# One V load ahead of the sums' weights, a copy moved to ScalarE, and another opening, in a fused attention and mixture kernel

## The chip, the core and the metric

The kernel runs on one NeuronCore of a Trainium2 chip. The core has five engines that run their own instruction streams and meet at semaphores: TensorE (PE in the profile; its weight loads are PEld), VectorE (DVE), ScalarE (ACT), GpSimd (POOL) and SyncE (SP). POOL and SP also issue DMA transfers. POOL's transfers go through one software queue (q0 in the profile), SP's through one hardware queue (q1); both run on the same 16 DMA engines. The metric is the device time of one execution in microseconds (us).

## The reference

Two stages are computed, the second from the first:

```python
# attention: 8 batches, 8 heads, 512 local and 32 global tokens, head size 64
out_g = softmax(q_g @ [k_g, k_l]^T / 8) @ [v_g, v_l]           # a global row sees everything
out_l = softmax([q_l @ k_g^T, q_l @ k_l^T within 32 rows] / 8) @ [v_g, v_l]
x = concat(out_g, out_l) as 4352 tokens x 512

# mixture: 8 experts, all of them for every token, weighted by P
P = exp(x @ w_gate - max)
8 times: P /= rows' sums; P /= columns' sums; P *= N / E
out = sum over e of P[:, e] * (relu(x @ w1[e]) @ w2[e])         # w1: 512 x 1024, w2: 1024 x 512
```

## The kernel before

**Slots.** Attention runs in 34 slots, s = 0 to 33 (the loop at L453). Slot s belongs to batch b = s // 4 and pair of heads hp = s % 4. Each slot issues pieces of several pairs in an order written out by hand, and each engine runs its own pieces in exactly that order:

- `st_A(s+1)` (L249) transposes q and k of the next pair on TensorE; VectorE copies k out of PSUM (`kTe`), ScalarE copies q (`qbd`).
- `st_B(s, part)` (L266), three parts: scores on TensorE, mask and row maximum on VectorE, exponential on ScalarE into `Pu`. Each row has 128 columns of a local window and 32 for the global tokens.
- `st_D1(s-1)` (L292): VectorE copies the 32 global columns of `Pu`, which lie strided, into `Pl` (L295); TensorE transposes the other 128; VectorE copies them to `pw` (L300).
- `st_D2` (L302): TensorE transposes `Pl`, and the finished rows `xn` of an earlier pair; ScalarE copies both out, the second into `xT`, the tokens for the mixture.
- `st_E(s-1)` (L319): probabilities times V on TensorE. Even blocks of 64 rows read `va`, odd ones `vb`, and the global part reads `vgz`.
- `st_G1` to `st_G4`: the same for the global rows.

From slot 5 on each slot also does a part of the mixture for experts 0 and 1: four pieces of the first layer (`p_l1`, L408) and from slot 8 two of the second (`p_l2`, L422). After each fourth piece of the second layer SP stores one megabyte (`yd<-yst`, L436). After the loop come the rest of experts 0 and 1, the balancing of P, and experts 2 to 7, computed with seven products of half size in place of eight (`Slot`, `Unit`); this last part takes from about 395 us to the end.

**V.** For each batch `load_v` (L152) returns five steps. The first loads the global V into DRAM as fp16 (`vg16`) and the first part of `va`; three more load `va[:, 1]` to `va[:, 3]`, all on POOL's queue; the last loads the end of `vb` and then issues, on SP's queue, three copies from `va` to `vb` (L166 to L168, the moves) and four small loads of `vgz` (`load_vz`, L150). The moves wait until what they read of `va` has landed, L167 for all four parts. `va`, `vb` and `vgz` have two buffers each, so batch b + 1 is loaded while batch b is computed; it is first needed at `st_E(4(b+1))`, in slot 4(b+1) + 1.

**The sums.** Experts 2 to 7 need sums and differences of blocks of their weights. In the 24 slots from 8 on, `sums_load` (L95) loads one weight matrix as fp16 (`pw`, 1 MB) in an even slot and `sums_form` (L102) forms four blocks on POOL in the odd slot after it (L113, four instructions) and stores them in DRAM (`kept<-psum`). There is one buffer `pw`, and POOL runs in order: load, wait, form, store, and so on. hp 0 and 1 have a first-layer matrix, hp 2 and 3 a second-layer one.

**The queue of loads.** The list `queue` holds steps for POOL. It is filled at hp 0 with four loads of the next batch's q and k, and at hp 2 with the five steps of V. From slot 8 on two steps are taken in hp 0 and in hp 1, three in hp 2 and the rest in hp 3. In hp 2 the sums' load is issued after the three steps, and in hp 3 the two last steps come before `sums_form`. So POOL's own order for a batch is: store of the sums, `vg`, three parts of `va`, `pw`, the fourth part of `va`, the end of `vb`, wait and form, store, q, k, `pw`, q, k, wait and form. Up to slot 7 everything in the queue is taken at once.

**The opening.** In slot 0 the global queries are cast (`cast_g`) and transposed (`transpose_g`, 4 products) before the second part of slot 0's scores is done. In slot 4 two pairs' rows `xn` are transposed, the second (`st_D2(None, 1)`, L524) ahead of `st_A(5)`.

Of the kernel before, what the change touches and what calls it, by code (L numbers as in the profile page):

```python
# [11 lines left out]
FP32 = mybir.dt.float32  # L12
# [11 lines left out]
def kernel(  # L24
# [13 lines left out]
    nc = tc.nc  # L38
# [5 lines left out]
    P = 128  # L44
# [5 lines left out]
    NJ = Sl // P  # L50
# [5 lines left out]
    KW = P  # L56
# [63 lines left out]
    with ExitStack() as att:  # L120
# [31 lines left out]
        def load_v(b):  # L152
            va, vb = vab[b % 2]
            vz = vgz[b % 2]
            src = v_l[b].rearrange("h s d -> s h d")

            def first():
                nc.gpsimd.dma_start(out=vg16[b], in_=v_g[b].rearrange("h g d -> g h d"))
                nc.gpsimd.dma_start(out=va[W:P, 0, :, 0:Dh], in_=src[0:96])

            def mid(j):
                nc.gpsimd.dma_start(out=va[:, j, :, 0:Dh], in_=src[P * j - W : P * j + 96])

            def last():
                nc.gpsimd.dma_start(out=vb[HB : HB + W, NJ - 1, :, 0:Dh], in_=src[Sl - W : Sl])
                nc.sync.dma_start(out=vb[96:P, NJ - 1], in_=va[W : 2 * W, 0])  # L166
                nc.sync.dma_start(out=vb[0:HB, :], in_=va[HB:P, :])  # L167
                nc.sync.dma_start(out=vb[HB:P, 0 : NJ - 1], in_=va[0:HB, 1:NJ])  # L168
                if b > 1:
                    load_vz(b)  # L170

            return [first] + [lambda j=j: mid(j) for j in range(1, NJ)] + [last]

        gst = {}

# [14 lines left out]
        def cast_g(tg):  # L190
            t, fv = gst[(0, tg)]
            nc.vector.tensor_copy(out=t, in_=fv)
            gst[(0, tg)] = t
# [55 lines left out]
        def st_A(n):  # L249
            b, hp = divmod(n, HP)  # L250
            qs, ks = staged[b]
            qb, kt = qbd[n % 2], kTe[n % 4]
            pt = ps_tr.tile([P, 2, Sl], FP16, tag="tr")
            for t, src in enumerate((ks, qs)):
                for so in range(NJ):
                    for a in range(2):
                        nc.tensor.transpose(pt[HB * a : HB * (a + 1), t, P * so : P * (so + 1)],  # L257
                                            src[:, 2 * hp + a, so, :], identity)
            nc.vector.tensor_copy(out=kt[:, W : W + Sl].rearrange("c (p s) -> c p s", s=NJ),
                                  in_=pt[:, 0, :].rearrange("c (s p) -> c p s", s=NJ))  # L260
            for a in range(2):
                r = slice(HB * a, HB * (a + 1))
                nc.scalar.copy(out=qb[r, :, HB * a : HB * (a + 1)].rearrange("c i (p s) -> c i p s", s=NJ),
                               in_=pt[r, 1, :].rearrange("c (s i p) -> c i p s", s=NJ, i=NHB))
# [27 lines left out]
        def st_D1(n):  # L292
            d = st[n]
            d["Pl"] = att_wk.tile([P, NHB, Sg], FP16, tag="Pl", name="Pl")
            nc.vector.tensor_copy(out=d["Pl"], in_=d["Pu"][:, :, KW:SW])  # L295
            ptw = ps_tr.tile([P, NHB, P], FP16, tag="tr")
            for i in range(NHB):
                nc.tensor.transpose(ptw[:, i, :], d["Pu"][:, i, 0:KW], identity)  # L298
            d["pw"] = att_wk.tile([P, NHB, P], FP16, tag="pw", name="pw")
            nc.vector.tensor_copy(out=d["pw"], in_=ptw)  # L300

        def st_D2(n, n2):  # L302
            tgx = ps_tr.tile([P, 6, P], FP16, tag="tr")
            if n2 is not None:
                b, hp = divmod(n2, HP)
                xn = st[n2]["xn"]
                for j in range(NJ):
                    nc.tensor.transpose(tgx[:, 2 + j, :], xn[:, j, :], identity)
            if n is not None:
                d = st[n]  # L310
                for t in range(2):
                    nc.tensor.transpose(tgx[:, t, :], d["Pl"][:, 4 * t : 4 * t + 4, :], identity)
                d["pg"] = att_wk.tile([P, 2, P], FP16, tag="pg", name="pg")
                nc.scalar.copy(out=d["pg"], in_=tgx[:, 0:2, :])
            if n2 is not None:
                nc.scalar.copy(out=xT[:, hp, Sl * b : Sl * (b + 1)], in_=tgx[:, 2:6, :].rearrange("p j q -> p (j q)"))
                del st[n2]
# [120 lines left out]
        def load_first():  # L438
            wts[0] = [load_w1(0)]
            nc.gpsimd.dma_start(out=wg_sb, in_=moe_w_gate.rearrange("(dko dki) e -> dki dko e", dki=P))  # L440

        queue = []
        NU = B * HP
        for t in range(2):
# [8 lines left out]
        for s in range(NU + 2):  # L453
            b, hp = divmod(s, HP)
            if s < NU and b + 1 < B:
                if hp == 0:
                    queue = load_qk(b + 1, 0, 4, H)
                if hp == 2:
                    queue += load_v(b + 1)
                if s == 4:  # L460
                    queue += [lambda: wts.__setitem__(1, [load_w1(1)]), lambda: wts[0].append(load_w2(0))]
                if s == 5:
                    queue += [lambda: load_g(1, "kgs"), lambda: load_g(1, "qgs")]
                if s == 7:
                    queue += [lambda: wts[1].append(load_w2(1))]
                take = 0 if s == 0 else len(queue) if s < 8 else 2 if hp < 2 else 3 if hp == 2 else len(queue)
                if s == 1:
                    queue += [load_first]
                    take = len(queue)
                for i, f in enumerate(queue[:take]):  # L470
                    f()
                    if s == 2 and i == 0:
                        load_vz(1)
                queue = queue[take:]

            if 8 <= s < 8 + 4 * (E - 2):
                i, late = divmod(s - 8, 2)
                (sums_form if late else sums_load)(2 + i // 2, i % 2)

            l1, l2 = [], []  # L480
            if s >= 5:
                pieces = range(4 * (s - 6) + 2, 4 * (s - 6) + 6)
                l1 = [(i // FT % 2, i // FT // 2, i % FT) if i >= 0 else None for i in pieces]
            if s >= 6:
                k, hf = divmod(s - 6, 2)
                if k >= 1:
                    l2 = [((k - 1) % 2, (k - 1) // 2, 2 * hf + i) for i in range(2)]
            n1 = n2 = 0

            def f1(eng):  # L490
                nonlocal n1
                if n1 < len(l1):
                    if l1[n1]:
                        p_l1(*l1[n1], eng)
                    n1 += 1

            def f2(eng):
                nonlocal n2
                if n2 < len(l2):
                    p_l2(*l2[n2], eng)  # L500
                    n2 += 1

            g_odd = s % 2 == 1 and 3 <= s <= NU + 1
            if g_odd:
                gb, gg = divmod((s - 3) // 2, 2)
            even = s % 2 == 0 and 2 <= s <= NU
            f1("a")
            if s < NU:
                st_B(s, 0)
            if even:  # L510
                st_G1(*divmod((s - 2) // 2, 2))
            if 1 <= s <= NU:
                st_D1(s - 1)
            if s == 3:
                st_E(1)
            if g_odd:
                st_G2(gb, gg)
            f2("a")
            if s < 7:
                st_B(s, 1)  # L520
            if 1 <= s:
                st_D2(s - 1 if s <= NU else None, s - 2 if s >= 4 else 0 if s == 3 else None)
            if s == 4:
                st_D2(None, 1)  # L524
            if 7 <= s < NU:
                st_B(s, 1)
            f1("a")
            if s + 1 < NU and s < 7:
                st_A(s + 1)
            if s == 0:  # L530
                cast_g("qgs")
                transpose_g(0, "qgs")
            f1("v")
            if s < NU:
                st_B(s, 2)
            if s + 1 < NU and s >= 7:
                st_A(s + 1)
            if s == 2:
                st_E(0)
            if 3 <= s <= NU:  # L540
                st_E(s - 1)
            f2("a")
            if s >= 6 and (s - 6) % 4 == 0:
                logits(NJ * ((s - 6) // 4), NJ)
            if g_odd:
                st_G3(gb, gg)
            if s == 8:
                transpose_g(1, "kgs")
                transpose_g(1, "qgs")
            if s == 18:  # L550
                st_G4(0)
            f1("a")
        logits(NJ * (B - 1), NJ)


# [445 lines left out]
```

## Time and profile before

| what | value |
|---|---|
| median of 3 runs | 1041.32 us (1039.04 to 1042.68) |
| the profiled execution | 1041.35 us, span 1039.6 us, mean granted clock 0.99 |
| PE busy | 997.0 us, 96% of the span |
| ACT, DVE busy | 654.7 us, 760.7 us |
| POOL busy | 260.9 us, 25% |
| q0 (POOL's queue) | 87.32 MB, 103776 packets |
| chain that ended last | PE 80%, DMA 9%, POOL 5% of the span |

The span is what the engines' records cover; the execution's own time has 1.75 us more around it. Busy time of PE counts pipelined products with modelled ends, so 96% does not mean that PE is at its peak. The waits say more: for each instruction they give what released it. The chain goes back from the last instruction, step by step, to whatever it had waited for.

### The profile page before, as it was taken

The page shows a single profiled execution, that of the slowest core. Times are in us where ns is not written, and L with a number is a line of the kernel's source. Part 1 is how long each engine was busy: PE and PEld are TensorE (multiplying, and loading weights), DVE is VectorE, ACT ScalarE, POOL GpSimd, SP SyncE. Part 2 cuts the span into 40 slices and gives each one's busy share as a digit, 9 for nine tenths or more (in the row PEclk, how much of TensorE's full clock was granted, in tenths as well). Part 3 has the DMA queues.
Part 4 walks back from the last instruction along what each step waited for, and adds up shares of the span by engine and source line. Part 5 has one row for each costly group of instructions (what it writes and reads, how often), then busy time and mean ns, then how long its engine had stood idle before and what let it go on. Part 6 is the DMA issues. An engine that isn't in the chain of part 4 may idle for free.

```text
span 1039.6 us, 21929 instructions
## 1 busy us (share of the span) xinstructions
PE 997.0 (96%) x8650; PEld 648.6 (62%) x8650; DVE 760.7 (73%) x1862; ACT 654.7 (63%) x1377; POOL 260.9 (25%) x280
## 2 busy tenths in 40 slices
PE   5899999997979999999999999999999999999997
PEld 3666556564545554666666666676767676676764
DVE  6765565654535273689999887898889999888785
ACT  6788888876756556775555555556775555555551
POOL 7335665646463322012011111111111111011000
PEclk9899999998989999999999999999999999999999
DMA  9999988889795658465463433356554433233043
GB/s 176 193 157 165 211 142 207 147 184 169 163 195 139 189 152 243 101 165 125 111 135 87 106 60 101 76 169 183 143 133 107 105 102 90 65 72 72 1 102 122
DMA packets 134376, 139.38 MB, mean 134 GB/s; under 512 B 54144, under 2 KB 107648, under 8 KB 130688
## 3 DMA queue, kind: packets, MB, share of 16 engines
q0 software_dynamic: 103776, 87.32, 47.7%
q1 hardware_dynamic: 29664, 50.27, 14.9%
q8 instruction: 67, 1.10, 0.4%
q10 hardware_dynamic: 832, 0.39, 0.1%
q14 instruction: 37, 0.30, 0.1%
HBM read 144.20 MB, written 39.58 MB: 177 GB/s over the span
## 4 chain that ended last, share of the span: by engine, by line
PE 80%; DMA 9%; POOL 5%; DVE 2%; issue 1%; ACT 1%; SPq 1%; POOLq 0%; ACTq 0%; DVEq 0%
PE z L728 29%; PE pa L823 17%; PE pb L823 8%; PE py L429 8%; PE ph L415 7%; DMA pw<-in_moe_w_dram 5%; PE pc L823 5%; POOL psum L113 3%; DMA va<-in_v_l_dram 3%; PE zp L794 1%; PE po L332 1%; DMA vb<-va 1%; PE pt L257 1%; PE sc L279 1%; PE ptw L298 1%
## 5 line engine op out<-in xcount | busy, mean ns | idle before, releaser
L728 PEld LDWEIGHTS <-hs 128*128 128x128 f16 x2264 | 220.7, 98 | 92.9 <-issue 1.1
L728 PE MATMUL z<-w2e,hs 128*128 128x256 f16 x1304 | 195.6, 273 | 0.9 <-DVE oy L762 0.9
L728 PE MATMUL z<-v,hs 128*128 128x256 f16 x960 | 144.0, 273 | 0.0
L429 PE MATMUL py<-w2e,hT 128*128 128x512 f16 x544 | 131.5, 387 | 0.3 <-DVE lg L404 0.3
L415 PE MATMUL ph<-xT,w1e 128*128 128x512 f16 (+1 forms) x576 | 129.9, 368 | 1.8 <-DVE lg L404 1.4
L749 ACT COPY z<-z 128x256 f32<-128x256 f32 x98 | 35.0, 357 | 141.7 <-PE z L728 141.7
L823 PEld LDWEIGHTS <-w1e 128*128 128x128 f16 x960 | 86.6, 97 | 59.1 <-issue 2.5
L286 DVE CUSTOM_DVE_ANT_0 ms<-sc,mask 128x160 f32<-128x160 f32 x256 | 69.9, 320 | 69.8 <-PE sc L281 65.5
L823 PE MATMUL pa<-t,s 128*128 128x512 f16 x384 | 114.2, 379 | 0.3 <-ACT s L848 0.3
L289 ACT ACTIVATE Pu<-ms,mx 128x160 f16<-128x160 f32 x256 | 92.2, 424 | 20.5 <-DVE mx L286 18.4
L762 DVE SCALAR_TENSOR_TENSOR oy<-z,lg,oy 128x512 f32<-128x512 f32 x128 | 95.8, 749 | 7.3 <-ACT oy L767 5.1
L724 DVE TENSOR_TENSOR hs<-hs 128x512 f16<-128x512 f16 x224 | 94.8, 423 | 8.2
L827 DVE CUSTOM_DVE_ANT_0 hx<-pb,s 128x512 f16<-128x512 f32 x96 | 65.9, 686 | 40.9 <-ACT s L857 30.1
L839 ACT ACTIVATE hs<-pc 128x512 f16<-128x512 f32 x96 | 57.2, 596 | 52.5 <-PE pc L823 52.5
L415 PEld LDWEIGHTS <-w1e 128*128 128x128 f16 x576 | 54.2, 98 | 53.1 <-issue 3.8
L827 DVE CUSTOM_DVE_ANT_0 hs<-pb,s 128x512 f16<-128x512 f32 x96 | 65.8, 686 | 27.1 <-ACT s L857 26.7
L644 POOL DMA_DIRECT2D w1e<-in_moe_w_dram x24 | 17.4, 730 | 271.8 <-PE pa L823 203.4
L113 POOL TENSOR_TENSOR psum<-pw 128x1024 f16<-128x1024 f16 x24 | 50.4, 2115 | 136.8 <-DMA pw<-in_moe_w_dram 136.8
L429 PEld LDWEIGHTS <-hT 128*128 128x128 f16 x544 | 50.7, 99 | 53.8 <-issue 3.7
L823 PEld LDWEIGHTS <-s 128*128 128x128 f16 x720 | 65.6, 98 | 29.2 <-issue 0.8
L644 POOL DMA_DIRECT2D w2e<-in_moe_w_dram x24 | 19.8, 831 | 240.4 <-PE z L728 235.0
L418 ACT ACTIVATE hT<-ph 128x512 f16<-128x512 f32 (+1 forms) x115 | 63.8, 567 | 18.4 <-PE ph L415 17.6
(182 smaller groups left out, 1928.8 us busy)
## 6 DMA issues: line engine op xcount, KB each, us to landing
ys<-yd SPq DMA_DIRECT2D x68, 256.0 KB, 3.4
yd<-yst SPq DMA_DIRECT2D x16, 1024.0 KB, 5.2
pw<-in_moe_w_dram POOLq DMA_DIRECT2D x12, 1024.0 KB, 12.9
kept<-psum POOLq DMA_DIRECT2D x12, 1024.0 KB, 4.9
s<-kept POOLq DMA_DIRECT2D x12, 768.0 KB, 8.8
v<-kept POOLq DMA_DIRECT2D x12, 768.0 KB, 8.9
w1e<-in_moe_w_dram POOLq DMA_DIRECT2D x12, 512.0 KB, 5.4
w2e<-in_moe_w_dram POOLq DMA_DIRECT2D x12, 512.0 KB, 6.6
```

Source lines behind the costliest of these rows:

```text
L113: nc.gpsimd.tensor_tensor(out=o, in0=x, in1=y, op=op)
L286: nc.vector.tensor_tensor_reduce(out=ms[:, ii, :], in0=sc[:, SW * ii : SW * (ii + 1)], in1=mask[:, mi, :], scale=-scale, scalar=BIG, op0=A ...
L289: nc.scalar.activation(out=d["Pu"][:, i, :], in_=ms[:, ii, :], func=AF.Exp, scale=-1.0, bias=d["mx"][:, i : i + 1])
L415: nc.tensor.matmul(ph[:, 0:n], wts[e][0][:, dk, P * fm : P * (fm + 1)], xT[:, dk, c0 : c0 + n], start=(dk == 0), stop=(dk == DP - 1))
L418: nc.scalar.activation(out=hT[:, fm, 0:n], in_=ph[:, 0:n], func=AF.Relu)
L429: nc.tensor.matmul(py, hT[:, fk, P * c : P * (c + 1)], wts[e][1][:, fk, :], start=(fk == 0), stop=(fk == FT - 1))
L724: nc.vector.tensor_tensor(out=o, in0=x, in1=y, op=op)
L728: nc.tensor.matmul(o, lhs[:, fk, :], rhs[:, fk, :], start=(first and fk == 0), stop=(fk == HF - 1), skip_group_check=True)
L762: nc.vector.scalar_tensor_tensor(out=o, in0=z, scalar=p, in1=o, op0=ALU.mult, op1=ALU.add)
L823: nc.tensor.matmul(o, lhs[:, dk, P * f : P * (f + 1)], rhs[:, dk], start=(first and n == 0 and dk == 0), stop=(dk == HD - 1), skip_group_c ...
L827: nc.vector._custom_dve(TENSOR_ADD_SAT, out=self.to(i, j), in0=self.of(ps), in1=self.of(s), s0=BIG, s1=0.0)
L839: nc.scalar.activation(out=self.to(0, 0), in_=self.of(self.pc), func=AF.Relu)
```

## The change

- V's load has six steps: the five without the three moves and `load_vz`, and a sixth, `move`, that holds them. All five loading steps are put in the queue at hp 2 and all are taken there, also from slot 8 on, so `pw` of hp 2 is issued after all of V. `move` is put at the head of the queue at hp 3.
- `Pl` is copied by ScalarE.
- In slots 1 to 4 nine products of 128 x 128 by 128 x 512 are added per slot, three after `st_D1` and six at the slot's end. Their result is never read.
- `st_D2(None, 1)` of slot 4 comes after `st_A(5)`; the transposes of the global queries come in slot 1, after `st_A(2)`; their cast stays in slot 0.

```diff
             def last():
                 nc.gpsimd.dma_start(out=vb[HB : HB + W, NJ - 1, :, 0:Dh], in_=src[Sl - W : Sl])
+
+            def move():
                 nc.sync.dma_start(out=vb[96:P, NJ - 1], in_=va[W : 2 * W, 0])
                 nc.sync.dma_start(out=vb[0:HB, :], in_=va[HB:P, :])
                 nc.sync.dma_start(out=vb[HB:P, 0 : NJ - 1], in_=va[0:HB, 1:NJ])
                 if b > 1:
                     load_vz(b)
-            return [first] + [lambda j=j: mid(j) for j in range(1, NJ)] + [last]
+            return [first] + [lambda j=j: mid(j) for j in range(1, NJ)] + [last, move]
...
-            nc.vector.tensor_copy(out=d["Pl"], in_=d["Pu"][:, :, KW:SW])
+            nc.scalar.copy(out=d["Pl"], in_=d["Pu"][:, :, KW:SW])
...
+        def keep_busy(n):
+            pm = ps_mm.tile([P, 512], FP32, tag="mm", name="pm")
+            for i in range(n):
+                nc.tensor.matmul(pm, identity, kgT[:, :, 0:P], start=True, stop=True)
...
                 if hp == 2:
-                    queue += load_v(b + 1)
+                    *loads, move = load_v(b + 1)
+                    queue += loads
+                if hp == 3:
+                    queue = [move] + queue
...
-                take = 0 if s == 0 else len(queue) if s < 8 else 2 if hp < 2 else 3 if hp == 2 else len(queue)
+                take = 0 if s == 0 else 2 if s >= 8 and hp < 2 else len(queue)
...
             if 1 <= s <= NU:
                 st_D1(s - 1)
+            if 1 <= s < 5:
+                keep_busy(3)
...
                 st_D2(s - 1 if s <= NU else None, s - 2 if s >= 4 else 0 if s == 3 else None)
-            if s == 4:
-                st_D2(None, 1)
...
             if s + 1 < NU and s < 7:
                 st_A(s + 1)
+            if s == 4:
+                st_D2(None, 1)
             if s == 0:
                 cast_g("qgs")
+            if s == 1:
                 transpose_g(0, "qgs")
...
             f1("a")
+            if 1 <= s < 5:
+                keep_busy(6)
```

## The prediction

> **What bounds the kernel now.** I read the waits of PE first, then the stretches around the longest, then the chain through one of them, then DMA issues by stretch. PE's waits, longest first (in all, times, longest, in us):
>
> ```profile
> PE po L332 <- DMA vb<-va: 12.0, 3, 5.6
> ...
> PE tgx L308 <- DVE pw L300: 3.5, 4, 1.2
> ...
> PE tgx L312 <- DVE Pl L295: 1.8, 3, 0.6
> ```
>
> Two of the three waits for `vb` are 5.6 and 5.1 us, at `st_E(24)` and `st_E(28)`, where batches 6 and 7 begin; small ones for `vgz` follow at once. Busy us and records of PE, PEld, DVE, ACT, POOL, then clock, DMA and GB/s, in four stretches:
>
> ```profile
> 220.00:240.00 20.00, 19.72 (x218) 11.78 (x218) 10.51 (x46) 16.23 (x37) 12.82 (x10) 1.00 0.68 139
> 240.00:260.00 20.00, 13.83 (x168) 8.13 (x163) 7.36 (x30) 10.22 (x23) 11.05 (x9) 0.86 1.05 165
> ...
> 280.00:300.00 20.00, 20.00 (x240) 11.98 (x236) 11.13 (x50) 16.58 (x38) 11.40 (x11) 1.00 0.93 136
> 300.00:320.00 20.00, 14.36 (x152) 8.37 (x149) 7.11 (x29) 9.02 (x21) 9.78 (x6) 0.83 0.78 213
> ```
>
> PE is full except in the second and fourth, where the granted clock falls too. The chain through the first wait (start, us, what):
>
> ```profile
> 235.64 0.49 POOL kept L114
> ...
> 236.22 0.46 POOL vg L158
> ...
> 239.34 0.86 POOL pw L98
> 240.20 11.28 DMA va<-in_v_l_dram
> ...
> 251.50 0.51 SPq L167
> ...
> 254.88 2.31 DMA vgz<-vg
> ...
> 257.23 0.77 PE po L332 x21
> ```
>
> The reader is to see that V's fourth part stands behind the sums' load, and that the chain before it is POOL's alone. POOL asked for V at 89.4, 136.6, 186.2, 236.2 and 286.4 us: 50 us per batch lately, while PE takes 42.5 (`st_E(20)` at 208.6, `st_E(24)` reached at 250.0, without a wait between). POOL loses 7 us per batch, and PE waits at the end of the last two. So the end is set by when batch 7's V is whole, 307.0 us; what PE saves before that is only waited away. Last, landing times of DMA issues (KB each, us), in 110 to 128, 209 to 228 and 236 to 252 us:
>
> ```profile
> pw<-in_moe_w_dram POOLq DMA_DIRECT2D x1, 1024.0 KB, 11.8
> ...
> pw<-in_moe_w_dram POOLq DMA_DIRECT2D x1, 1024.0 KB, 15.0
> yd<-yst SPq DMA_DIRECT2D x1, 1024.0 KB, 10.1
> ...
> va<-in_v_l_dram POOLq DMA_DIRECT2D x3, 128.0 KB, 6.1
> vb<-va SPq DMA_DIRECT2D x1, 260.0 KB, 3.1
> vb<-va SPq DMA_DIRECT2D x1, 32.5 KB, 5.6
> ```
>
> The first-layer `pw` lands in 11.8 us when no store `yd` meets it (batch 3), in 14.7, 15.0 and 15.6 when one does (batches 4 to 6).
>
> **V, from its request to its last piece.** In batch 6 that was 236.2 to 257.2 us. Now the fourth part goes out at 239.3, where `pw` did; its three forerunners landed 6.1 us after issue, so it lands at 245.5, 6.0 us sooner. The moves and `vgz` then took 5.7 us with the queues empty; now they run beside `pw`. The only move that did so before, the one of 32 KB, took 5.6 us against 3.1 for one of 260 KB that ran alone: 2.5 to 2.8 lost, once, since the rest queue behind it in order. Gain 6.0 - 2.8 = 3.2 us; the ends are 6.0 (no loss) and 0 (the moves move only when `pw` is through).
>
> The Trainium skill, DMA: Bandwidth & Descriptors, "Queues, rings and completion order", says that each DMA engine takes its queues in turn, a packet at a time. By that the moves would start at once and `pw` would pay for their bytes, which is rival C, 1044.3 us by the rule; the small move's 5.6 us speaks for a wait instead.
>
> **The sums' load.** All that was asked for with V had landed by 251.5 us, `pw` at 250.0; `pw` is now last, so lands at 251.5: 1.4 us later. The moves beside it carry 0.6 MB; a store of 1 MB alone lands in 4.1 us, so they cost it 0 to 2.4; I take 0.3, since they come when it is nearly through. So 1.7 us per batch (1.1 to 3.8). Behind it on POOL wait form, store, next q, k and `pw`, and the next V. Four such slips lie ahead of batch 7's request, three ahead of batch 6's. POOL's one wait for PE there, 0.5 us at batch 3's V, goes, since PE saves two waits for `pw` or `Pl`, 0.6 and 1.0 us, at 52 and 59 us.
>
> **The store that meets the other load.** SP's order does not change. In batch 5 the sums' store before the first-layer `pw` went out at 209.6 us, `yd` at 211.8. Three slips less 0.5 put the first at 214.2; `yd` follows PE and lands alone in 4.1 us, by 215.9, before `pw` moves: 15.0 becomes 11.8, 3.2 saved. Batch 6: V is asked for at +5.1 - 0.5 - 3.2 = +1.4, whole at +1.4 - 3.2 = -1.8, so PE goes on 1.8 sooner and `yd` goes out at 260.3 (262.05 before); the sums' store moves from 259.1 to 262.2 (+6.8 - 0.5 - 3.2). They overlap for about 1 us of the 3.8 that this `pw` loses: 2.8 saved. Batch 4's `yd` comes 9 us after its store, and still meets `pw`. If neither is spared, 6.0 us more.
>
> **Batch 7.** Request +6.8 - 0.5 - 3.2 - 2.8 = +0.3, whole at -2.9. PE reaches it at 300.3 - 1.8 = 298.5 and still waits some 5 us, so this is the end's own shift.
>
> **The copy of `Pl`.** On VectorE:
>
> ```profile
> L295 DVE COPY Pl<-Pu x32: 216/222/2155, 15.4 to 337.5; 128x256 f16<-128x256 f16 x32
> ```
>
> 222 ns, or up to 2155 while POOL forms sums (2115 ns an instruction). On ScalarE the nearest row is `pg`, of the same shape, 378 ns: 32 x 0.38 = 12 us more for an engine at 16 of 20 us. Hidden before batch 7's wait. After it one gap falls away, 1.2 us for `pw` at 327.6; in slots 30 and 32 `Pl` queues behind three exponentials and the long one (0.71 us) and may hold PE 0.2 us each: -0.8 in all (0.8 later to 1.2 sooner).
>
> [...]
>
> **The opening.** 36 products at 216 ns (eight of this width take 1.73 us in the chain) are 7.8 us of PE, at half clock 15.3 (8 took 3.40). PE idles 6.5 us in slots 1 to 4 (1.7, 1.3 and 1.7 the largest, for `qbd`, `vb` and `xT`), and from 39 to 46 us its clock is 0.52, about 3 us of work lost, which more work before may keep. The last of these is what the reorder in slot 4 takes away, since `st_A(5)` no longer stands behind two pairs' copies. So PE stands about even at slot 6 (1 us sooner to 3 later), and POOL's loads of that time wait for DMAs, not for PE; batch 3's V alone asks PE. Priced at nothing; if the cover fails, rival D. The transposes and the moves of slots 2 and 6 cost nothing: POOL's and SP's orders up to slot 7 stay.
>
> **Sum.** -2.9 - 0.8 = -3.7 us, on the profiled execution's 1041.35 (its span 1039.6 and 1.75 around it; the median is 1041.32): 1037.7 us.
>
> **Rivals.**
> A, the forecast: 1037.7, with its own ends 1034 to 1041.
> B, V gains more: the moves lose nothing beside `pw` (2.8 more), and PE's last wait shrinks to some 2 us, so that the clock holds. The cold restart costs 1.7 us in `py` (3.60 against 1.89) and 0.6 in the products at L376 and L377 behind it: 1037.7 - 2.8 - 2.3 = 1032.6. The falling clock after each wait speaks for it; that small move against.
> C, slower: moves and sums' load take turns, and the load pays for every byte of the moves, 3.8 us per batch in place of 1.7. Four times 2.1 more is 8.4, less 1.8 for moves that then lose only about 1 us of the 2.8 (an estimate, 2.4 us of work stretched by under a half): 1044.3. It decides once the slip is above some 2.6 us with the stores spared, 1.1 without; with 1.7 and no store spared it is 1043.7 as well. POOL has no slack to absorb it, which speaks for it.
> D, slower: the added products run at half clock and delay slot 8 by 15.3 - 6.5 - 1.6 = 7.2 us; batch 3's V waits for PE by as much, and all after it: 1037.7 + 0.5 + 7.2 = 1045.4. It decides from 3.2 us on. PE's records in slot 3 leave about 1 us idle, which speaks for it; its clock of 1.00 from 29 to 39 us against.
> E, nothing: V is whole no sooner, since the moves wait for `pw` to end, and spared stores pay for the slip: about 1041.
>
> **How the numbers follow.** About 0.3%, 3.1 us, is what a measurement of this kernel can tell from no change. A has 0.44, of which 0.30 below 1038.2 us; B 0.15; C 0.25, of which 0.16 above 1044.4, where a store is not spared either; D 0.12, of which 0.11 above; E 0.04. Faster 0.30 + 0.15 = 0.45; slower 0.16 + 0.11 = 0.27; within 0.14 + 0.09 + 0.01 + 0.04 = 0.28. The range 1032 to 1046 takes in A to E and leaves out some 2 in 10: more slips than four of 3.8, or both waits gone.
>
> **What would show it.** In the profile after, L167 follows V's request by 9 us, not 15; `vgz` lands 17 to 18 us after it; second-layer `pw` lands about 1.7 us later after the request; first-layer `pw` of batches 5 and 6 lands in about 12 us; PE's waits for `vb` at batches 6 and 7 stay, ending near 256 and 304 us; no gap for `pw` at 325; the clock holds from 39 to 46 us. I am wrong if first-layer loads still take 15 us, if the slip is over 2.6 us, or if batch 3's V waits for PE by microseconds.

## The result, and the profile after

The changed kernel takes 1043.92 us (median of 13 runs, 1041.09 to 1045.81) against 1039.72 us for the kernel before (13 runs, 1035.54 to 1042.68). The ratio is 1.0039, with a 95% interval of 1.0025 to 1.0053: slower by 4 us, where 3.7 us faster had been forecast. The profiled execution after took 1043.95 us, its span is 1042.2 us.

PE's waits after (us in all, times, longest):

```profile
PE po L334 <- DMA vb<-va: 11.6, 3, 5.7
...
PE tgx L314 <- ACT Pl L297: 4.8, 6, 1.8
...
PE tgx L310 <- DVE pw L302: 1.5, 2, 0.9
```

The three waits for `vb` are still there and as long as before. They end later: the last piece of batch 7's V landed at 306.9 us before and lands at 311.1 us now. Of the four stretches the second and the fourth (the columns as before the change):

```profile
240.00:260.00 20.00, 14.77 (x164) 8.68 (x163) 8.74 (x36) 14.66 (x35) 7.96 (x9) 0.99 1.16 194
...
300.00:320.00 20.00, 13.81 (x133) 7.91 (x132) 6.65 (x27) 9.60 (x23) 9.42 (x6) 0.83 0.86 196
```

These two are still the thin ones; batch 6's wait has moved to the end of its stretch (254.6 to 259.8 us), so the clock falls behind it. The chain through batch 7's wait (start, us, what) shows that what was to become quicker did. First the last piece before, then the chain after:

```profile
304.67 2.27 DMA vgz<-vg
```

```profile
293.08 0.46 POOL vg L158
...
296.18 6.17 DMA va<-in_v_l_dram
...
302.49 0.51 SPq L169
...
306.26 4.82 DMA vgz<-vg
```

The sums' load is out of the chain, L169 follows the request of V by 9.3 us (forecast 9), and the last piece is there 18.0 us after the request where it was 20.6. That is a gain of 2.6 us, 3.2 forecast. But the request itself stands at 293.1 us, not at 286.4. Where it was lost, the lines of the sums' loads show: L98 issues the second-layer loads, L100 the first-layer ones, and under each stands who waited for it (us in all, times). Before, and then after:

```profile
L98 POOL DMA_DIRECT2D pw<-in_moe_w_dram x6: 893/909/920, 93.1 to 333.4; - x6
  POOL psum L113: 58.0, 6
...
L100 POOL DMA_DIRECT2D pw<-in_moe_w_dram x6: 760/780/814, 60.9 to 309.7; - x6
  POOL psum L113: 78.7, 6
```

```profile
L98 POOL DMA_DIRECT2D pw<-in_moe_w_dram x6: 909/924/932, 93.1 to 339.7; - x6
  POOL psum L113: 70.6, 6
...
L100 POOL DMA_DIRECT2D pw<-in_moe_w_dram x6: 760/780/817, 59.9 to 319.6; - x6
  POOL psum L113: 70.5, 6
```

Over all twelve loads the change traded 8.2 us of POOL's waits for first-layer loads against 12.6 us for second-layer ones, and a second-layer load is issued 1.4 us later per batch besides: 4.54 us after V's request in batches 4 to 7, 3.1 before. Batch by batch, the time from V's request to the sums' store was 23.65, 23.36, 23.32 and 22.84 us in batches 3 to 6; it is 29.21, 25.28, 24.91 and 26.16 us. The slips are 5.6, 1.9, 1.6 and 3.3 us, 12.4 in all, where the forecast had four times 1.7. Landing times (KB each, us) after, in 92 to 112, 219 to 236 and 270 to 286 us:

```profile
pw<-in_moe_w_dram POOLq DMA_DIRECT2D x1, 1024.0 KB, 15.1
...
vb<-va SPq DMA_DIRECT2D x1, 260.0 KB, 6.1
```

```profile
pw<-in_moe_w_dram POOLq DMA_DIRECT2D x1, 1024.0 KB, 13.0
```

```profile
pw<-in_moe_w_dram POOLq DMA_DIRECT2D x1, 1024.0 KB, 12.4
```

The last two are the first-layer loads of batches 5 and 6: they are spared most of the stores, as forecast. The first fence is batch 3, with the largest slip, 5.6 us: its load, from 93.1 to 108.1 us, runs beside the moves and meets, early on, a store of `yd` as well, which went out at 89.8 us and landed at 97.2.

### The profile page after: what moved, and what is told of

Its sections match the earlier page's. It is cut to its first block, busy times and chain, and to the rows that moved or that the text cites. A ratio compares the mean times of both kernels' runs of the same rounds, so it can differ in the third digit from the quotient of the medians.

```text
span 1042.2 us, 22002 instructions
## 1 busy us (share of the span) xinstructions
PE 999.8 (96%) x8686; PEld 647.2 (62%) x8686; DVE 750.1 (72%) x1830; ACT 662.3 (64%) x1409; POOL 260.8 (25%) x280
## 3 DMA queue, kind: packets, MB, share of 16 engines
q1 hardware_dynamic: 29664, 50.27, 14.8%
## 4 chain that ended last, share of the span: by engine, by line
PE 84%; DMA 5%; DVE 3%; POOL 3%; ACT 2%; issue 2%; SPq 0%; ACTq 0%; DVEq 0%; POOLq 0%
PE z L743 29%; PE pa L838 17%; PE ph L417 9%; PE pb L838 8%; PE py L431 8%; PE pc L838 5%; DMA pw<-in_moe_w_dram 2%; POOL psum L113 2%; DMA va<-in_v_l_dram 1%; PE zp L809 1%; PE po L334 1%; DVE ms L288 1%; PE pt L259 1%; PE sc L281 1%; DMA vb<-va 1%
## 6 DMA issues: line engine op xcount, KB each, us to landing
pw<-in_moe_w_dram POOLq DMA_DIRECT2D x12, 1024.0 KB, 12.4
```

## Experiments

Each is compared with the kernel before, run beside it on the same chip. In the first four, S is the theory that batch 7's V sets the end and the loss comes from the opening, whose lateness pushes the first store into batch 3's loads; P, that PE's lateness in the opening goes straight to the end; V, that V ahead delays the sums' load by more per batch than it brings. A time is the median of many executions; waits, slips and landings are read from the trace of one.

### V's part alone

```diff
-            return [first] + [lambda j=j: mid(j) for j in range(1, NJ)] + [last]
+            return [first] + [lambda j=j: mid(j) for j in range(1, NJ)] + [last, move]
...
-                    queue += load_v(b + 1)
+                    *loads, move = load_v(b + 1)
+                    queue += loads
+                if hp == 3:
+                    queue = [move] + queue
```

> The kernel before with V's part of the change alone. In the changed kernel PE came to slot 8 4.4 us later than before, and the first yd store, at 89.8 in place of 85.3 us, met batch 3's V and sums' load, which landed 20.3 us after V's request in place of 14.7. Theory S (the end is set by when batch 7's V is whole; the loss came because the late opening pushed the first store into batch 3's loads): without the opening the first store stays near 85 us, batch 3's sums' load lands 16 to 17 us after V's request, and the kernel is 2 to 4 us faster than before. Theory P (the opening's lateness of PE goes to the end by itself): 0 to 3 us faster. Theory V (putting V ahead delays the sums' load in every batch by more than it brings): 2 to 5 us slower than before.

1042.18 us (12 runs) against 1038.23 (35 runs), ratio 1.0035 (1.0012 to 1.0059). The loss is here without the opening, as large as in the whole change within the intervals; S and P fall as its cause. (That batch 7's V sets the end, the other half of S, stands.) POOL's waits for second-layer and for first-layer loads:

```profile
  POOL psum L113: 67.9, 6
  POOL psum L113: 70.4, 6
```

The slips are 2.9, 1.9, 1.7 and 3.4 us, 9.9 in all. In batches 5 and 6 the first-layer loads are formed 12.7 and 11.5 us after issue (15.1 and 15.8 before), 6.7 us spared; the loads of batches 3 and 4 gained nothing (12.1 and 16.0; 11.9 and 14.8 before). Batch 7's request comes 4.7 us later, and V is whole 18.4 us after it.

### The copy alone

```diff
-            nc.vector.tensor_copy(out=d["Pl"], in_=d["Pu"][:, :, KW:SW])
+            nc.scalar.copy(out=d["Pl"], in_=d["Pu"][:, :, KW:SW])
```

> The kernel before with the copy of Pl on ScalarE alone. Theory S: PE is later at slot 8 by 1 to 3 us, because ScalarE is the busy engine in slots 4 to 6 and Pl stands behind the exponentials; POOL's requests for V move by under 1 us, one gap of 1.2 us goes after batch 7's V, so -1.5 to +1 us. Theory P: 1 to 3 us slower.

1039.71 us, ratio 1.0003 (0.9983 to 1.0024): no change that can be measured. PE waits for it early in the kernel:

```profile
PE tgx L312 <- ACT Pl L295: 5.9, 7, 1.8
```

That is 5.9 us where VectorE's copy had 1.8, but in time that is waited away at batch 6. In this trace the first store goes out at 88.0 us, not 85.3, and meets batch 3's loads: a slip of 1.9 us there without V's change. Batch 4's first-layer load, formed 12.4 us after its issue and not 14.8, gives it back.

### The opening alone

```diff
+            if 1 <= s < 5:
+                keep_busy(3)
...
-            if s == 4:
-                st_D2(None, 1)
...
+            if s == 4:
+                st_D2(None, 1)
...
+            if s == 1:
                 transpose_g(0, "qgs")
...
+            if 1 <= s < 5:
+                keep_busy(6)
```

> The kernel before with the opening alone (36 unread products, the two reorders). Theory S: PE 1 to 3 us later at slot 8; the first store at 86 to 88 us runs into the sums' store and batch 3's V, batch 3's sums' load lands 1 to 3 us later after V's request, later stores may be spared: -1 to +3 us. Theory P: 1 to 3 us slower, as much as PE is late at slot 8.

1038.13 us, ratio 1.0003 (0.9978 to 1.0027): no change. The clock did hold here, and only in part in the whole change. From 39 to 46 us, before the change, with the opening alone and after (the clock is the third figure from the end):

```profile
39.00:46.00 7.00, 6.36 (x93) 5.14 (x88) 5.09 (x22) 5.38 (x14) 1.15 (x2) 0.52 1.16 233
```

```profile
39.00:46.00 7.00, 4.78 (x98) 3.71 (x94) 4.72 (x25) 5.93 (x16) 1.15 (x2) 1.00 1.19 231
```

```profile
39.00:46.00 7.00, 5.97 (x89) 4.04 (x88) 3.17 (x14) 4.41 (x12) 1.15 (x2) 0.76 1.14 224
```

The clock is 1.00 in place of 0.52 with the opening alone and 0.76 in the whole change. Whether the products or the two reorders hold it, no run separates. It brings nothing, since PE waits for POOL later on.

### V and the copy

```diff
-                    queue += load_v(b + 1)
+                    *loads, move = load_v(b + 1)
...
-            nc.vector.tensor_copy(out=d["Pl"], in_=d["Pu"][:, :, KW:SW])
+            nc.scalar.copy(out=d["Pl"], in_=d["Pu"][:, :, KW:SW])
```

> The changed kernel without the opening: V's part and the copy. Theory S: between the two alone; the first store at 86 to 88 us, batch 3's sums' load 16 to 20 us after V's request; -3 to +2 us. Theory P: later than V's part alone by the copy's share of PE's lateness, 1 to 3 us. Theory V: 2 to 5 us slower than before.

The diff is an excerpt; the edit is all of V's part, and the copy. 1043.15 us, ratio 1.0045 (1.0028 to 1.0063). Together with the three before: V's part is the loss, whatever stands beside it.

### V in one go for batch 7 alone

The edit is shown against V's part alone.

```diff
+                    if 8 <= s < 26:
+                        loads[4:] = [lambda end=loads[4], move=move: (end(), move())]
                     queue += loads
-                if hp == 3:
+                if hp == 3 and (s < 8 or s > 26):
                     queue = [move] + queue
...
-... 2 if s >= 8 and hp < 2 else len(queue)
+... 2 if s >= 8 and hp < 2 else 3 if s >= 8 and hp == 2 and s < 26 else len(queue)
```

> The kernel before, with V loaded in one go and its moves a slot later for batch 7 alone (and batches 1 and 2, as before); batches 3 to 6 keep the old order. Theory T (a trade): the end is set by when batch 7's V is whole; asking for V in one go makes it whole 3.0 us sooner after its request, but holds the sums' load back by 1.6 to 3.4 us in every batch, and four such slips stand ahead of batch 7's request. Here none of the four slips is left, since the one that remains comes behind the last request: request of batch 7 where it was before (286 us in the profile, give or take 1.5), V whole 17.6 us after it (20.6 before), 3.0 us faster than before, ratio 0.997. Theory R (the loss lies elsewhere: V's early transfers or the moves' place cost by themselves, and nothing is gained at batch 7): no faster, or slower by about 1 us, a quarter of the loss.

1037.24 us against 1039.53 (27 runs), ratio 0.9975 (0.9958 to 0.9993): 2.3 us faster, 3.0 forecast. V is whole 18.1 us after a request at 285.2 us; the 17.6 and the gain of 3.0 us in the expectation counted V's last loads short, 18.4 and 2.2 are right for V's part alone. So the gain at the end is real, 2.5 us here, and the slips of the four batches ahead of it turned it into a loss. R falls.

### The moves behind the sums' load

The edit is shown against V's part alone. The read waits for the load to land, and SP's moves stand behind it.

```diff
             def move():
+                if b > 2:
+                    nc.sync.dma_start(out=seen, in_=work["w"][0:1, 0, 0:16])
```

> V's part alone, and SP reads 32 bytes of the sums' load before each batch's moves (batches 3 to 7), so the moves wait until that load has landed and share nothing with it. Theory T1 (of the slip, 1.4 us is the later issue of the sums' load, the rest is bytes of the moves and of vgz beside its end): the forming starts 10.8 to 11.3 us after the load is issued, as before (11.5 to 12.8 with V's part alone), the slips are 1.4 to 1.6 us in place of 1.6 to 3.4, batch 7's request comes 1 us later than before, not 4.7; but V is whole some 21 us after its request, no sooner than before, so the time is 0 to 2 us above before. Theory T2 (the slip comes from V's own bytes ahead of the load in POOL's queue; the moves cost it nothing): forming still 11.5 to 12.8 us after the issue, request as late as with V's part alone, V whole 3 us later than there: 6 to 7 us above before.

1045.01 us, ratio 1.0051 (1.0032 to 1.0069). On the slip T1 has the mechanism, though its 1.4 to 1.6 us are 0.2 to 1.9: the second-layer loads are formed 10.3, 10.7, 10.1 and 11.3 us after their issue (12.6, 11.8, 11.5 and 12.8 with V's part alone), so what SP sends beside a load costs it 1.1 to 2.3 us, 1.6 in the mean. Single traces vary, but the difference is not one trace's: in all five traces with V ahead and the moves beside the load, it is formed 11.0 to 13.1 us after its issue in batches 4 to 6, 11.9 in the mean, against 10.7 here. The slips shrink from 9.9 to 3.5 us, 0.9 per batch, though the load is still issued 1.4 us later after V's request than before. The read holds back, with the moves, the store of `yd` behind them, which with V's part alone also meets the end of the load (in batch 6 it goes out at 255.7 us, and the load lands at 259.0). The moves are enough without it: in the kernel after with held stores (below) the load is formed 13.1, 11.8 and 11.9 us after its issue in batches 4 to 6. On the time T1 was wrong by at least 3.5 us (5.5 above before, 0 to 2 forecast), and T2's time was nearer for another reason than its own. The first-layer loads of batches 4 to 6 take 15.7 us each, so no store is spared: in batch 6 the store behind the moves on SP goes out at 260.7 us, and the next follows PE, which V held until 262.4 us, at 266.7, just as that load does. What the slip gave, the stores took, and V was whole no sooner after its request (21.7 us).

### The sums' load ahead of V

```diff
+                if s >= 8 and hp == 2:
+                    sums_load(2 + (s - 8) // 4, 1)
                 for i, f in enumerate(queue[:take]):
...
-                (sums_form if late else sums_load)(2 + i // 2, i % 2)
+                if late or hp == 0 or b + 1 >= B:
+                    (sums_form if late else sums_load)(2 + i // 2, i % 2)
```

> The kernel before, with the second-layer sums' load issued ahead of all of V in the slots of hp 2 (the change's reorder turned round); the moves stay where they are in the program. Theory T: the load is asked for 3.1 us sooner after the sums' store, so POOL's chain is 3.1 us shorter in each of four batches, 12 us sooner at batch 7's request; V is whole 2 to 3 us later after it (23 to 24 us from the load's issue). Together 6 to 10 us sooner; PE's waits at batches 6 and 7, 11.4 us in all, shrink to 2 to 5 us, and the clock recovers for some of it: 1030 to 1034, ratio 0.991 to 0.995. Theory R (what a load ahead of another saves, the other loses; the sum over a batch is set by bytes, not by order): batch 7's V whole no sooner, 1038 to 1041.

1047.26 us, ratio 1.0069 (1.0047 to 1.0092): 7.7 us slower, which neither theory had. POOL's waits, in the same order:

```profile
  POOL psum L113: 48.8, 6
  POOL psum L113: 93.2, 6
```

The second-layer loads pay 9.2 us less than before, as T says; the first-layer loads pay 14.5 us more. V behind the load lands later, so the moves go later, and the store of `yd` that stands behind them on SP goes out with the sums' store. Both stores of a batch now meet the first-layer load. In 262 to 284 us:

```profile
yd<-yst SPq DMA_DIRECT2D x2, 1024.0 KB, 7.4
kept<-psum POOLq DMA_DIRECT2D x1, 1024.0 KB, 8.6
pw<-in_moe_w_dram POOLq DMA_DIRECT2D x1, 1024.0 KB, 18.0
```

It lands in 18.0 us beside two stores, 15 beside one, 12 beside none. Which stores a load meets decides more than the order of the loads.

### After, with its first store later

The edit is against the kernel after.

```diff
+                f = lambda: nc.sync.dma_start(out=yd[e][m], in_=ys[:, 0:nt, :])
+                first_store.append(f) if (e, m) == (0, 0) else f()
...
+                if s == 11:
+                    first_store.pop()()
```

> The kernel after, with the first megabyte stored from the mixture's second layer (89.8 us in the profile after) held on SP until behind batch 3's moves, some 14 us later. In the profile after it meets batch 3's V and sums' load, whose forming starts 15.2 us after its issue (12.6 with V's part alone, where that store comes at 85.4 us). Theory C (that meeting is a part of the loss that only the whole change has): forming 12 to 13 us after the issue, batch 4's request 2 to 3 us sooner (138 to 139 us), time 1.5 to 3 us less than after. Theory N (the copy and the opening cost nothing, as they did alone, and a later slip or store takes this back): within 1 us of after, 1042.9 to 1044.9.

1041.87 us, ratio to before 1.0024 (1.0004 to 1.0045), where after has 1.0039. In the trace, batch 3's load is formed 12.7 us after its issue, not 15.2, and batch 7 is requested at 291.3 us, not 293.1, so C holds there. In the time it is 1.5 in a thousand, and the two intervals overlap: of the right size, but not shown by the times alone.

### Stores held until the sums' load has landed

```diff
+                if "w" in work and m < 6:
+                    nc.sync.dma_start(out=seen, in_=work["w"][0:1, 0, 0:16])
                 nc.sync.dma_start(out=yd[e][m], in_=ys[:, 0:nt, :])
```

The same edit was put into the kernel before, into the one with V in one go for batch 7 alone, and into the kernel after.

> The kernel before, and ahead of each megabyte stored from the mixture's second layer in slots 9 to 31 SP reads 32 bytes of the sums' load, so a store never runs beside that load, only beside the forming. Nothing of V is changed. Theory T (the end is set by POOL's chain of loads, and what that chain costs beyond its own bytes is the meeting with these stores): the first-layer loads of batches 4, 5 and 6 are formed 12 us after their issue, not 14.8, 15.1 and 15.8; 9 to 10 us in all, batch 7's request at 276 to 278 us, PE's waits at batches 6 and 7 (11.4 us) nearly gone, and the clock held: 1028 to 1032, ratio 0.990 to 0.993. Theory R (as with the sums' load ahead of V, what one meeting gives another takes: the held store meets V, the moves or the sums' store): within 3 us of before.

> Held stores, and V in one go for batch 7 alone. Theory T: as held stores alone, and batch 7's V 3 us sooner after its request; with PE reaching batch 7 at about 294 us, V comes about when PE does, so at most 1 to 3 us below held stores alone: 1026 to 1030. Theory R: 1034 to 1038, as V in one go for batch 7 alone.

> The kernel after with held stores. Theory T: the loss of the change is the slips of the second-layer load, 12.4 us in the profile after, less the stores that it spares the first-layer load; holding the stores gives both kernels the same first-layer loads (12 us), so after gains only 4 to 5 us by it (batch 4's 15.4, batch 5's 13.1 and batch 6's 12.6 become 12) where before gains 9 to 10: 1038 to 1041, 8 to 10 us slower than before with held stores. Theory R (the change's loss has nothing to do with POOL's chain): as far above before with held stores as after is above before, 4 us.

The times without held stores are those of the sections above, each beside its own runs of before.

| kernel | without held stores | with held stores | ratio to before, with held stores |
|---|---|---|---|
| before | 1039.12 us | 1032.24 us | 0.994 (0.9917 to 0.9963) |
| V in one go, batch 7 alone | 1037.24 us | 1026.51 us | 0.988 (0.986 to 0.990) |
| after | 1043.92 us | 1039.69 us | 1.0007 (0.9992 to 1.0022) |

In the kernel before the first-layer loads of batches 4 to 6 now take 12.9, 13.0 and 12.3 us, and batch 7 is requested at 280.1 us, not 286.4: the time is just above T's 1028 to 1032, the request later than the 276 to 278 forecast. The change costs 7.5 us on top of it, just under the forecast 8 to 10: with nearly the same first-layer loads in both, the slips are left, 12.7 us in the last kernel's trace against the first row's, and batch 7 is requested 10.8 us later. Of that 5.8 us fall on batch 3, whose loads still meet the first store: it goes out at 89.4 us, before the load is issued at 94.4, so its read does not wait for that one. Rival R said 4. The second row beats both kernels, and lies 5.7 us below the first, where 1 to 3 had been forecast. Its second and fourth stretch:

```profile
240.00:260.00 20.00, 18.30 (x186) 10.72 (x185) 11.55 (x43) 14.86 (x34) 12.78 (x10) 1.00 0.89 192
...
300.00:320.00 20.00, 19.72 (x232) 11.52 (x230) 10.95 (x45) 15.05 (x36) 9.27 (x6) 1.00 0.58 159
```

and its waits for `vb`:

```profile
PE po L334 <- DMA vb<-va: 1.9, 2, 1.1
```

PE is all but full in the fourth, its clock is whole, and of the waits for `vb` at batches 6 and 7 none is left (the two in this line are at 25 and 48 us; one of 0.7 us for `vgz` remains at batch 6).

## Why the prediction was wrong

**What bounds the kernel** was right: the end follows batch 7's V. In the ten traces without held stores V's last piece lands anywhere from 303.3 to 314.1 us, and the span ends 730 to 733 us behind it in each. Another opening and another copy changed nothing, holding stores changed 7 us, and V in one go at the end alone changed 2.3. One reading was off without effect on the sum: from 208.6 to 250.0 us PE takes 41.4 us for a batch, not 42.5, so POOL loses 8.6 us per batch, not 7.

**V, from its request to its last piece** was right in mechanism and near in size: 3.1 us gained in batch 6, from whose rows the 3.2 came, and 2.6 in batch 7, the one that counts. There V's fourth part landed 5.5 us sooner after the request (6.0 forecast), and the moves and `vgz` took 8.7 us beside the load, 5.8 before; 2.5 to 2.8 us more had been taken.

**The sums' load: the failed step.** The load is issued 1.4 us later, as said, but with the moves out of the way the slips are only 0.2 to 1.9 us, 0.9 in the mean: the 1.4 was somewhat too much. The 0.3 us for the moves beside the load was far too little: that term is 1.1 to 2.3 us, 1.6 in the mean, by the difference between V's part with and without the moves in the way, inside the 0 to 2.4 that the text itself gave for their bytes. It had been argued that the load is nearly through when the moves come. But in batch 7 after, V's last part has landed at 302.4 us, when the load, issued at 297.6 and through at 310.0, has more than half its way to go. In batch 3 of the whole change a store comes on top, another 2.5 us by the trace with the first store later. So the slips are 9.9 us with V alone and 12.4 in the whole change, not 6.8. The text's own bound of 3.8 per batch would have held all but that one, and its condition, slower once the slip is above 2.6 us, was met by the mean of 3.1; with V's part alone the mean is 2.5, and it lost as much. Rival C had the mechanism and nearly the time, 1044.3, the latter in part by luck: its slip of 3.8 per batch was too high (15.2 us in all, 9.9 and 12.4 measured), and so was the 5.0 us that it let V gain (2.6 measured).

The rule from the Trainium skill (DMA: Bandwidth & Descriptors, "Queues, rings and completion order"), that a DMA engine takes its queues in turn, came nearer than the row that the forecast preferred: both sides paid, the 260 KB move 6.1 us in place of 3.2 in batch 3, and the load 1.6 us in the mean.

**The store that meets the other load** was right for batches 5 and 6: 2.0 and 3.2 us spared (3.2 and 2.8 forecast), 2.4 and 4.3 with V alone. That batch 4's load would still meet its store was said, and it does; that it would take longer was not: it is formed 0.7 us later after its issue, 1.2 with V alone.

**POOL's wait for PE** at batch 3's V, 0.5 us: there was none to go. The same 0.5 us stand in the trace after, ahead of V and as issue.

**Sum.** With the slips as measured, the request of batch 7 comes 6.7 us later (forecast 0.3): 12.4 of slips and 0.3 and 0.7 at the first-layer loads of batches 3 and 4, less 5.2 at those of 5 and 6 and 1.5 that batch 3's request comes sooner. Less 2.6 for V, its last piece lands 4.1 us later. Behind it PE needs 1.5 us less, which leaves 2.6 us, the difference of the two spans (1042.2 and 1039.6). The difference of the medians is 4.2, since the profiled execution of before is one of its slower ones.

**The copy**: behind batch 7's wait the gap of 1.2 us for `pw` went, as forecast, and one of 0.2 for `Pl` came. That is 1.0 us less. The products right behind the wait, where the clock is low, took 0.9 less (3.5 and 0.9 us in the chain before, 3.1 and 0.4 after), and smaller differences take 0.4 back. In the times, -0.8 us is below what these runs can tell from nothing.

**The opening** was priced at nothing, and alone it is nothing, though the clock held from 39 to 46 us only in part in the whole change (0.76). Rival D was half right: in the whole change PE comes 4.7 us later to `st_E` of slot 9. The same group in the chain, before and after (start, us, what):

```profile
92.83 0.51 PE po L332 x32
```

```profile
97.56 0.51 PE po L334 x32
```

Batch 3's V did not wait for it; the first store did, and so came into batch 3's loads, at 89.8 us in place of 85.3. The copy has the larger share of this: alone it brings the store to 88.0 us, the opening alone to 86.4. The 2.5 us that this adds to batch 3's slip were put at nothing: the forecast asked whether POOL waits for PE there, and not what SP's store, which follows PE, meets.

## What to carry to other kernels

A load that is moved ahead of another on one queue moves everything behind it in every turn of the loop, and gains only at the turn that ends last: count the slip once per turn, and make the change in the last turn alone. A transfer that becomes free to start earlier is not free for its new neighbour; its bytes at the neighbour's rate are the price to reckon with until a row shows less (up to 2.4 us by that here, 1.1 to 2.3 measured). Where stores that nobody waits for run on another queue beside a load that everybody waits for, hold them with a read of a few bytes of the loaded tile, and check what stands behind that read in its queue.

## What was not expected of the hardware

- A store of 1 MB on SP's queue lands in 4.1 us alone. Beside a load of POOL's queue it landed in 10.1 us and cost that load some 3 us (11.8 against 14.7 to 15.6 in the kernel before); two stores cost it 6 us (18.0, with the sums' load ahead of V).
- A read of 32 bytes of the tile being loaded is enough to order SP's queue behind POOL's: with nothing else changed, the kernel took 6.9 us less, ratio 0.994.
- With nine products of which nothing is read in each of four slots, and two reorders, the granted clock was 1.00 where it was 0.52 (from 39 to 46 us, the opening alone); with the copy and V's part besides it was 0.76. The time shows neither a cost nor a gain, since PE waits 200 us later for POOL.
